# Decode attention over a key-value cache: scores as 16 rows of 512 keys, with the query as padded weight columns

## The chip, the cores and the metric

The kernel runs on one core of one Trainium2 chip. The metric is the device time in microseconds of one execution. Names of engines: PE is the tensor engine (PEld its weight loads), DVE the vector engine, ACT the scalar engine, POOL the general-purpose engine, SP the engine whose queue issues the transfers.

## What is computed

Eight sequences (B = 8) have one new token each. The model has a width of 640, 32 heads of 128 and a cache of 4096 keys and values per head. Two identical rounds (called layers 0 and 1 here) are run over the same cache:

```python
x = x + _A_ref(_layernorm(x), A_k_cache, A_v_cache, A_wq, A_wo)
x = x + _B_ref(_layernorm(x), B_w1, B_w2)
x = x + _A_ref(_layernorm(x), A_k_cache, A_v_cache, A_wq, A_wo)
x = x + _B_ref(_layernorm(x), B_w1, B_w2)
# _A_ref: q = x @ wq;  p = softmax(q . k / sqrt(128)) over 4096 keys;  o = p . v;  o @ wo
# _B_ref: relu(x @ w1) @ w2, inner width 1728
```

Everything is bf16 in memory. The cache is 537 MB; each layer needs all of it.

## The kernel before

**Visits.** A visit is one pair of heads (hp, 16 pairs) of one sequence b in one layer: 256 visits. Each has a K tile and a V tile, and each tile consists of four units (g = 0 to 3) of 512 KB, 4 KB per partition. On the chip an arena of G = 26 units holds them. For each sequence the kernel finishes layer 0, and later returns to it for layer 1; of the 128 units of a sequence, 21 stay in the arena between the two layers (the plan calls them kept) and two more are stashed in PSUM, so that layer 1 need not load them again.

**The plan.** Nothing is scheduled by a compiler. `plan()` writes out one list of operations in advance, and each engine's instructions stand in the order of that list. The order of tiles is K of visit 0, then K of visit i+1 and V of visit i in turn. Between the units of a tile, `step()` puts in small pieces of other work (chains): the softmax of a visit (T, M2, B, E, L, I), its output projection (OC, OG, O, W, Y), the rest of the layer (`finish`: norm, up, relu, down, add, norm) and the next queries (Q, QC). Where a tile can't start without a piece, `until()` puts that piece ahead of it. `feed()` writes a load into the list as soon as enough units of the arena have been given back; a load takes 1 to 8 units, depending on how far ahead the loads are by the plan's own clock. All loads go through SP's queue (L478).

**The turn.** When the last visit of layer 0 of a sequence has been done, its `finish` chain runs beside four visits of the next sequence (AHEAD = 4); then come the visits of layer 1, which start with heads 15, 14 and 13, the kept ones. While the kept units lie in the arena, five units are left for the four visits, and every load there is of one unit. There are seven such turns, one per sequence but the last.

**Scores.** A unit of K before holds 2048 keys of one head as 16 blocks of 128 keys. Each block is a weight load of 128x128 and a matmul with one column, q (L524), so the scores of a visit are a 128x64 tile, one PSUM half of `s_ps` per visit by turns. The maximum goes over the free axis (M1, L530), is transposed by a matmul with the identity (T, L534), reduced again and put on a 2x2 diagonal (M2, L538 and L540), and spread over the partitions by a matmul (B, L543). E is a scaled copy (L547) and one Exp per head (L551), which writes P as the 128x64 columns that the V matmuls need as weights. L (L556) sums P by a matmul with ones, I (L562, L566) inverts it.

**Values.** A unit of V is four matmuls with four weight columns of P each and 512 moving columns, in the four column groups of the array (`tile_position=(0, 32 * c)`, L512). Rows 32c to 32c+3 of `o_ps` hold the result; a copy (OC, L570), four matmuls that pick the right rows (OG, L575) and a scaling by 1/L (O, L585) follow.

Of the kernel before, what the change touches and what calls it, by code (L numbers as in the profile page):

```python
# [9 lines left out]
FP32 = mybir.dt.float32  # L10
# [7 lines left out]
GP = 4  # L18
# [14 lines left out]
def plan(B, NP, n_up, n_down):  # L33
# [29 lines left out]
    for i in range(NV + 1):  # L63
        pair = [("K", i)] * (i < NV) + [("V", i - 1)] * (i >= 1)
        slots += pair[::-1] if i and visits[i - 1][0] == 0 and last_of[visits[i - 1][:2]] == i - 1 else pair
    stream = []
    for which, i in slots:
        layer, b, hp = visits[i]
        stream += [(which, i, g) for g in range(UNIT) if layer == 0 or (which, hp, g) not in keep]

# [11 lines left out]
    where, kept, ready = {}, {}, {}  # L82
    ops, chains = [], []
    at = [0, 0]
# [65 lines left out]
    def take(c):  # L150

        n, op = c.pop(0)
        if op:
            ops.append(op)
            clock[0] += 0.1 + 0.03 * n
        while c and not c[0][0]:
            ops.append(c.pop(0)[1])

    def step():
# [14 lines left out]
    def query(b, n):  # L174

        return [(10, ("Q", b, order1[n])), (0, ("QC", b, order1[n]))]

    def finish(layer, b):

        norm = [(0, "sums"), (2, "mean"), (0, "center"), (2, "var"), (0, "scale"), (1, None), (1, None)]  # L180
        c = norm + [(15, ("up", k)) for k in range(n_up)] + [(0, "relu")]
        c += [(14, ("down", k)) for k in range(n_down)] + [(0, "add")]
        if layer == 0:
            c += norm
        c = [(n, op and ("C", layer, b, k, op)) for k, (n, op) in enumerate(c)]
        if layer == 0:
            c += query(b, 0) + query(b, 1)
        return c

    feed()  # L190
    for which, i in slots:
        layer, b, hp = visits[i]
        if which == "K":
            if layer == 0 and b == 0 and hp % GP == 0:
                ops.append(("Q0", hp // GP))
            if layer:
                until(("QC", b, hp))
                if order1.index(hp) + 2 < NP:
                    chains.append(query(b, order1.index(hp) + 2))
        else:  # L200
            until(("E", i))
            clock[0] = max(clock[0], ready.pop(i))
        for g in range(UNIT):
            u = find(which, i, g)
            ops.append(("mm", which, i, g, u))
            clock[0] = max(clock[0], lands[u]) + 0.5
            release(which, i, g)
            if g + 1 < UNIT:
                step()
        if which == "K":  # L210
            ops.append(("M1", i))
            ready[i] = clock[0] + 3
            step()
            chains.append([(1, ("T", i)), (0, ("M2", i)), (1, ("B", i)), (0, ("E", i)), (1, None), (1, ("L", i)), (0, ("I", i))])
        else:
# [24 lines left out]
def kernel(  # L240
# [25 lines left out]
    GW = W // UNIT  # L266
    GJ = GW // P
    VJ = NJ // UNIT
# [48 lines left out]
    nc.vector.memset(onesb_c, 1.0)  # L317
    ones_b = _free(onesb_c[:2], [(0, P)])
    ones_p = _free(onesb_c, [(0, P)])
# [3 lines left out]
    for c in range(4):  # L323
        rows = slice(32 * c, 32 * c + CJ)
        nc.vector.tensor_copy(out=gsel[rows, :, c // 2], in_=ident[rows, rows])
    eps_c = consts.tile([P, 1], FP32, name="eps_c")
    nc.vector.memset(eps_c, eps)
# [6 lines left out]
    o_ps = ps.tile([P, CJ * Dh], FP32, name="o_ps")  # L334
    s_ps = ps.tile([P, 2, 2 * NJ], FP32, name="s_ps")
    blk_ps = ps.tile([P, BANK], FP32, name="blk_ps")
# [6 lines left out]
    visits, ops = plan(B, NP, len(up_parts), DC)  # L343
    q1, s_tiles, P_tiles, m_tiles, o_tiles, blk, oy, invL, oT, nmax, st = ({} for _ in range(11))

# [160 lines left out]
    def do_mm(which, i, g, u):  # L506
        layer, b, hp = visits[i]
        at = u * GW
        if which == "V":
# [7 lines left out]
            return  # L517
        if g == 0:
            s_tiles[i] = s_ps[:, i % 2]
        h = 2 * hp + g * 2 // UNIT  # L520
        q = q1[b][:, h : h + 1] if layer else q0[:, h, b : b + 1]
        for n in range(GJ):
            j = g * GJ + n
            nc.tensor.matmul(  # L524
                s_tiles[i][:, j : j + 1], lhsT=arena[:, at + n * P : at + (n + 1) * P], rhs=q, start=True, stop=True
            )

    def do_m1(i):
        m_tiles[i] = sm.tile([P, 2], BF16, name="mrow")
        nc.vector.tensor_reduce(out=m_tiles[i], in_=s_tiles[i].rearrange("p (h j) -> p h j", h=2), axis=AX.X, op=ALU.max)  # L530

    def do_t(i):
        blk[i] = blk_ps[:, : P + 2 + 2 * NJ]
        nc.tensor.matmul(blk[i][:2, :P], lhsT=m_tiles.pop(i), rhs=ident, start=True, stop=True)  # L534

    def do_m2(i):
        hmx = sm.tile([2, 1], FP32, name="hmx")
        nc.vector.tensor_reduce(out=hmx, in_=blk[i][:2, :P], axis=AX.X, op=ALU.max)  # L538
        nmax[i] = sm.tile([2, 2], BF16, name="diag")
        nc.vector.tensor_tensor(out=nmax[i], in0=ident[:2, :2], in1=_free(hmx, [(0, 2)]), op=ALU.mult)  # L540

    def do_b(i):
        nc.tensor.matmul(blk[i][:, P : P + 2], lhsT=ones_b, rhs=nmax.pop(i), start=True, stop=True)  # L543

    def do_e(i):
        nm = sm.tile([P, 2], FP32, name="nmax")
        nc.scalar.activation(out=nm, in_=blk[i][:, P : P + 2], func=ACT.Copy, scale=-inv_sqrt_dh)  # L547
        P_tiles[i] = sm.tile([P, 2, NJ], BF16, name="P_sb", bufs=3)
        S = s_tiles.pop(i).rearrange("p (h j) -> p h j", h=2)
        for h in range(2):  # L550
            nc.scalar.activation(  # L551
                out=P_tiles[i][:, h, :], in_=S[:, h, :], func=ACT.Exp, bias=nm[:, h : h + 1], scale=inv_sqrt_dh
            )

    def do_l(i):
        nc.tensor.matmul(  # L556
            blk[i][:, P + 2 :], lhsT=ones_p, rhs=P_tiles[i].rearrange("p h j -> p (h j)"), start=True, stop=True
        )

    def do_i(i):  # L560
        L = sm.tile([P, 2], FP32, name="lsum")
        nc.vector.tensor_reduce(  # L562
            out=L, in_=blk.pop(i)[:, P + 2 :].rearrange("p (h j) -> p h j", h=2), axis=AX.X, op=ALU.add
        )
        invL[i] = sm.tile([P, 2], FP32, name="invL", bufs=3)
        nc.vector.reciprocal(out=invL[i], in_=L)  # L566

# [29 lines left out]
    def do_y(i):  # L597
# [5 lines left out]
    does = dict(load=do_load, stash=do_stash, unstash=do_unstash, weights=load_weights, mm=do_mm, M1=do_m1, T=do_t, M2=do_m2, B=do_b, E=do_e,  # L603
                L=do_l, I=do_i, OC=do_oc, OG=do_og, O=do_o, W=do_w, Y=do_y, C=do_finish, Q0=do_q0, Q=do_q, QC=take_q)

# [16 lines left out]
def _laid_out(A_x, A_k_cache, A_v_cache, A_wq, A_wo, B_w1, B_w2):  # L622
# [8 lines left out]
    w2[:Dff] = B_w2  # L631
    k = A_k_cache.reshape(B, NP, 2, Sk, Dh).transpose(0, 1, 4, 2, 3).reshape(B, NP, Dh, 2 * Sk)
    v = A_v_cache.reshape(B, NP, 2, UNIT, NJ // UNIT, p, Dh).transpose(0, 1, 5, 3, 2, 4, 6).reshape(B, NP, p, -1)
# [38 lines left out]
```

## Time and profile before

| | |
|---|---|
| runs before (3) | 2372.81, 2374.57, 2378.23 us; median 2374.57 |
| profiled execution | 2376.09 us, its span 2374.3 us |
| PE busy | 1292.5 us (54% of the span), 26486 matmuls and as many weight loads |
| DVE, ACT, POOL busy | 377.7, 355.9, 42.8 us |
| bytes moved | 996.04 MB, mean 420 GB/s |
| granted PE clock | 1.00 |

The span runs from the first to the last instruction of the core; some 1.8 us lie outside it. Busy times of engines overlap. The tables of waits say what ended the idle time of an engine, not that this time counts.

### The profile page before, as it was taken

To read this page: it belongs to the slowest core of one execution; us is meant where nothing else is said; L and a number is where in the kernel's file an instruction comes from. 1 tells how busy PE (TensorE), PEld (TensorE's weight loads), DVE (VectorE), ACT (ScalarE), POOL (GpSimd) and SP (SyncE) were. 2 spreads that over 40 slices of the span, in tenths; PEclk is the share of its full clock that TensorE was granted. 3 is DMA by queue.
4 is the path that set the end of the run, shared out by engine and by line. 5 is a ranking of instruction groups with operands and counts; after the bars stand their busy time and mean duration, and the time that the engine had idled before them with its cause. 6 is when DMAs were issued, how large, how long until landed. Compare 5 with 4: busy or idle time off the path is not lost.

```text
span 2374.3 us, 57948 instructions
## 1 busy us (share of the span) xinstructions
PE 1292.5 (54%) x26486; PEld 783.7 (33%) x26486; DVE 377.7 (16%) x1840; ACT 355.9 (15%) x1195; POOL 42.8 (2%) x198
## 2 busy tenths in 40 slices
PE   3436644476445754458454574446744466545845
PEld 2324322243223532225222352223422244223523
DVE  1102111121111211112111121112211112112211
ACT  1111211111111211112111121111211112111211
POOL 0000000000000000000000000000000000000000
DMA  9999999999999999999999999999999999999997
GB/s 411 428 429 403 428 432 431 429 398 433 428 433 427 391 433 428 433 423 404 430 434 433 406 401 431 433 431 408 420 431 430 430 408 417 431 432 410 405 434 302
DMA packets 92794, 996.04 MB, mean 420 GB/s; under 512 B 10372, under 2 KB 10372, under 8 KB 54916
## 3 DMA queue, kind: packets, MB, share of 16 engines
q1 hardware_dynamic: 92548, 992.33, 99.1%
q8 instruction: 207, 3.39, 0.5%
q14 instruction: 39, 0.32, 0.0%
HBM read 992.27 MB, written 0.01 MB: 418 GB/s over the span
## 4 chain that ended last, share of the span: by engine, by line
DMA 81%; PE 14%; DVE 2%; ACT 2%; issue 1%; POOL 1%; SPq 0%; POOLq 0%; DVEq 0%; ACTq 0%
DMA arena<-in_A_kv_dram 81%; PE o_ps L512 5%; PE s_ps L524 5%; ACT o_sb L570 1%; DVE hmx L538 1%; PE oy_ps L575 1%; PE blk_ps L496 1%; PE blk_ps L543 1%; DVE diag L540 0%; PE oy_ps L592 0%; PE blk_ps L534 0%; PE oy_ps L434 0%; DMA wq_sb<-in_A_wq_dram 0%; DVE arena L475 0%; POOL root L399 0%
## 5 line engine op out<-in xcount | busy, mean ns | idle before, releaser
L512 PE MATMUL o_ps<-arena,P_sb 128*4 128x512 bf16 x4096 | 564.8, 599 | 373.9 <-DMA arena<-in_A_kv_dram 371.6
L524 PEld LDWEIGHTS <-arena 128*128 128x128 bf16 x16384 | 501.6, 105 | 667.0 <-DMA arena<-in_A_kv_dram 660.7
L524 PE MATMUL s_ps<-q_96,arena 128*128 128x1 bf16 x8192 | 275.2, 166 | 371.9 <-DMA arena<-in_A_kv_dram 360.0
L547 ACT ACTIVATE nmax<-blk_ps 128x2 f32<-128x2 f32 x256 | 44.0, 172 | 1638.3 <-PE blk_ps L543 1638.3
L512 PEld LDWEIGHTS <-P_sb 128*4 128x4 bf16 x4096 | 90.6, 81 | 442.5 <-issue 429.4
L570 ACT CAST o_sb<-o_ps 100x512 bf16<-100x512 f32 x256 | 149.8, 585 | 228.8 <-PE o_ps L512 228.8
L562 DVE TENSOR_REDUCE lsum<-blk_ps 128x2 f32<-128x64 f32 x256 | 57.3, 224 | 588.6 <-PE blk_ps L556 588.6
L530 DVE TENSOR_REDUCE mrow<-s_ps 128x2 bf16<-128x64 f32 x256 | 57.5, 224 | 578.1 <-PE s_ps L524 542.6
L551 ACT ACTIVATE P_sb<-s_ps,nmax 128x32 bf16<-128x32 f32 x512 | 118.8, 283 | 8.2
L538 DVE TENSOR_REDUCE hmx<-blk_ps 2x1 f32<-2x128 f32 x256 | 71.4, 279 | 207.2 <-PE blk_ps L534 207.2
L556 PEld LDWEIGHTS <-onesb_c 128*128 128x128 bf16 x256 | 26.4, 103 | 199.7 <-issue 199.7
L585 DVE TENSOR_TENSOR oT<-oy_ps,invL 128x2 bf16<-128x2 f32 x128 | 20.4, 160 | 350.5 <-PE oy_ps L575 350.5
L575 PE MATMUL oy_ps<-gsel,o_sb 100*128 100x2 bf16 x1024 | 66.1, 168 | 17.5 <-ACT o_sb L570 0.7
L534 PE MATMUL blk_ps<-ident,mrow 128*2 128x128 bf16 x256 | 70.0, 274 | 3.1 <-DVE mrow L530 3.1
L543 PEld LDWEIGHTS <-onesb_c 2*128 2x128 bf16 x256 | 25.1, 98 | 125.1 <-issue 125.0
L556 PE MATMUL blk_ps<-P_sb,onesb_c 128*128 128x64 bf16 x256 | 59.7, 233 | 0.0
L575 PEld LDWEIGHTS <-o_sb 100*128 100x128 bf16 x1024 | 47.4, 106 | 33.6 <-ACT o_sb L570 29.6
L524 PE MATMUL s_ps<-q_22833,arena 128*128 128x1 bf16 x1024 | 34.1, 166 | 43.6 <-DMA arena<-in_A_kv_dram 43.4
L524 PE MATMUL s_ps<-q_18821,arena 128*128 128x1 bf16 x1024 | 33.9, 166 | 43.4 <-DMA arena<-in_A_kv_dram 43.3
L524 PE MATMUL s_ps<-q_2773,arena 128*128 128x1 bf16 x1024 | 33.9, 166 | 42.7 <-DMA arena<-in_A_kv_dram 42.7
L524 PE MATMUL s_ps<-q_14809,arena 128*128 128x1 bf16 x1024 | 34.1, 166 | 42.4 <-DMA arena<-in_A_kv_dram 41.9
L524 PE MATMUL s_ps<-q_10797,arena 128*128 128x1 bf16 x1024 | 33.9, 166 | 42.6 <-DMA arena<-in_A_kv_dram 42.5
(179 smaller groups left out, 781.2 us busy)
## 6 DMA issues: line engine op xcount, KB each, us to landing
arena<-in_A_kv_dram SPq DMA_DIRECT2D x109, 4096.0 KB, 24.8
arena<-in_A_kv_dram SPq DMA_DIRECT2D x100, 2048.0 KB, 25.2
arena<-in_A_kv_dram SPq DMA_DIRECT2D x348, 512.0 KB, 6.2
arena<-in_A_kv_dram SPq DMA_DIRECT2D x16, 2560.0 KB, 22.6
arena<-in_A_kv_dram SPq DMA_DIRECT2D x35, 1024.0 KB, 12.8
arena<-in_A_kv_dram SPq DMA_DIRECT2D x17, 1536.0 KB, 24.4
arena<-in_A_kv_dram SPq DMA_DIRECT2D x6, 3072.0 KB, 23.3
wq_sb<-in_A_wq_dram SPq DMA_DIRECT2D x4, 1280.0 KB, 30.0
```

Of the source, the lines that this page charges most:

```text
L512: nc.tensor.matmul(o_ps[32 * c : 32 * c + CJ, :], lhsT=P_tiles[i][:, h, j : j + CJ], rhs=arena[:, at + c * CJ * Dh : at + (c + 1) * CJ * D ...
L524: nc.tensor.matmul(s_tiles[i][:, j : j + 1], lhsT=arena[:, at + n * P : at + (n + 1) * P], rhs=q, start=True, stop=True)
L530: nc.vector.tensor_reduce(out=m_tiles[i], in_=s_tiles[i].rearrange("p (h j) -> p h j", h=2), axis=AX.X, op=ALU.max)
L534: nc.tensor.matmul(blk[i][:2, :P], lhsT=m_tiles.pop(i), rhs=ident, start=True, stop=True)
L538: nc.vector.tensor_reduce(out=hmx, in_=blk[i][:2, :P], axis=AX.X, op=ALU.max)
L543: nc.tensor.matmul(blk[i][:, P : P + 2], lhsT=ones_b, rhs=nmax.pop(i), start=True, stop=True)
L547: nc.scalar.activation(out=nm, in_=blk[i][:, P : P + 2], func=ACT.Copy, scale=-inv_sqrt_dh)
L551: nc.scalar.activation(out=P_tiles[i][:, h, :], in_=S[:, h, :], func=ACT.Exp, bias=nm[:, h : h + 1], scale=inv_sqrt_dh)
L556: nc.tensor.matmul(blk[i][:, P + 2 :], lhsT=ones_p, rhs=P_tiles[i].rearrange("p h j -> p (h j)"), start=True, stop=True)
L562: nc.vector.tensor_reduce(out=L, in_=blk.pop(i)[:, P + 2 :].rearrange("p (h j) -> p h j", h=2), axis=AX.X, op=ALU.add)
L570: nc.scalar.copy(out=o_tiles[i][:OR], in_=o_ps[:OR, :].rearrange("p (j d) -> p j d", j=CJ))
L575: nc.tensor.matmul(oy[i][:, :2], lhsT=o_tiles[i][:OR, j, :], rhs=gsel[:OR, j, :], start=(j == 0), stop=(j == CJ - 1))
```

## The change

Each K unit now holds 1024 keys of both heads (`_laid_out` orders the cache so on the host), as four blocks of 512 keys: two of head 0, two of head 1. The query is the weight and K moves: for each unit and block a matmul with four weight columns, of which column g is q and the other three are zero, adds into rows 32c to 32c+3 of one PSUM bank, so that after four units row 32c+g holds 512 scores. The four columns are a window into an 8-column buffer `qz` with q in column 3; POOL writes q there once per visit (`QZ`, three buffers). The maximum and Exp go over 16 rows of 512 keys (on 100 partitions, of which the others hold nothing of use); four matmuls with a selection matrix `rsel` (`PT`) turn P into the 128x64 columns of before, and a DVE copy (`PC`) takes them out of PSUM. `s_ps` is one bank instead of two halves by turns, so that K of visit i+1 is put behind E of visit i. At a turn the K and V tiles alternate by halves where the V tile came first before.

The core of the diff:

```diff
-        pair = [("K", i)] * (i < NV) + [("V", i - 1)] * (i >= 1)
-        slots += pair[::-1] if i and visits[i - 1][0] == 0 and last_of[visits[i - 1][:2]] == i - 1 else pair
+        turn = i and visits[i - 1][0] == 0 and last_of[visits[i - 1][:2]] == i - 1
+        for gs in (range(UNIT // 2), range(UNIT // 2, UNIT)) if turn else (range(UNIT),):
+            slots += [("K", i, gs)] * (i < NV) + [("V", i - 1, gs)] * (i >= 1)
...
+            pad(i)
+            if i + 1 < NV and (visits[i + 1][0] or b or hp % GP != GP - 1):
+                pad(i + 1)
+            until(("E", i - 1))
+        elif gs[0] == 0:
+            until(("PC", i))
             clock[0] = max(clock[0], ready.pop(i))
...
-            chains.append([(1, ("T", i)), (0, ("M2", i)), (1, ("B", i)), (0, ("E", i)), (1, None), (1, ("L", i)), (0, ("I", i))])
+            chains.append([(1, ("T", i)), (0, ("M2", i)), (1, ("B", i)), (0, ("E", i)), (1, None),
+                           (2, ("PT", i)), (0, ("PC", i)), (1, ("L", i)), (0, ("I", i))])
...
-        for n in range(GJ):
-            j = g * GJ + n
+        for c in range(4):
             nc.tensor.matmul(
-                s_tiles[i][:, j : j + 1], lhsT=arena[:, at + n * P : at + (n + 1) * P], rhs=q, start=True, stop=True
+                s_ps[32 * c : 32 * c + CJ, :], lhsT=qz[:, i % 3, c // 2, 3 - g : 3 - g + CJ],
+                rhs=arena[:, at + c * BANK : at + (c + 1) * BANK],
+                start=(g == 0), stop=(g == UNIT - 1), tile_position=(0, 32 * c),
             )
...
+        nc.gpsimd.tensor_copy(out=qz[:, i % 3, :, 3], in_=q)
...
-        nc.vector.tensor_reduce(out=m_tiles[i], in_=s_tiles[i].rearrange("p (h j) -> p h j", h=2), axis=AX.X, op=ALU.max)
+        nc.vector.tensor_reduce(out=m_tiles[i][:OR], in_=s_ps[:OR], axis=AX.X, op=ALU.max)
...
-        nc.tensor.matmul(blk[i][:2, :P], lhsT=m_tiles.pop(i), rhs=ident, start=True, stop=True)
+        nc.tensor.matmul(blk[i][:1, : 4 * CJ], lhsT=m_tiles.pop(i)[:OR], rhs=rsel[:OR], start=True, stop=True)
...
-        nc.vector.tensor_tensor(out=nmax[i], in0=ident[:2, :2], in1=_free(hmx, [(0, 2)]), op=ALU.mult)
...
+        for h in range(2):
+            nc.tensor.matmul(
+                blk[i][64 * h : 64 * (h + 1), 16:17], lhsT=ones_h, rhs=mx[:, h : h + 1], start=True, stop=True,
+                tile_position=(0, 64 * h),
+            )
...
-        for h in range(2):
-            nc.scalar.activation(
-                out=P_tiles[i][:, h, :], in_=S[:, h, :], func=ACT.Exp, bias=nm[:, h : h + 1], scale=inv_sqrt_dh
+        nc.scalar.activation(out=P_rows[i][:OR], in_=s_ps[:OR], func=ACT.Exp, bias=nm[:OR], scale=inv_sqrt_dh)
+
+    def do_pt(i):
+        P_row = P_rows.pop(i)
+        for k in range(BANK // P):
+            nc.tensor.matmul(
+                blk[i][:, 32 + k * 4 * CJ : 32 + (k + 1) * 4 * CJ], lhsT=P_row[:OR, k * P : (k + 1) * P],
+                rhs=rsel[:OR], start=True, stop=True,
             )
+
+    def do_pc(i):
+        P_tiles[i] = sm.tile([P, 2, NJ], BF16, name="P_sb", bufs=2)
+        nc.vector.tensor_copy(
+            out=P_tiles[i].rearrange("p h (c k) -> p h c k", k=BANK // P),
+            in_=blk[i][:, 32 : 32 + 2 * NJ].rearrange("p (k h c) -> p h c k", k=BANK // P, h=2),
+        )
```

## The prediction

> **What bounds the kernel now.** I read the page first: the queues and the chain that ended last.
>
> ```profile
> DMA packets 92794, 996.04 MB, mean 420 GB/s; under 512 B 10372, under 2 KB 10372, under 8 KB 54916
> q1 hardware_dynamic: 92548, 992.33, 99.1%
> q8 instruction: 207, 3.39, 0.5%
> DMA 81%; PE 14%; DVE 2%; ACT 2%; issue 1%; POOL 1%; SPq 0%; POOLq 0%; DVEq 0%; ACTq 0%
> ```
>
> The kernel is bound by its transfers: the data's packets fill 99.1% of sixteen engines' span, and no compute engine is above 54%. The change moves no byte of the cache more or less, so at first sight it should do nothing. The third line is the one that matters. Queue q8 brings instructions: 3.39 MB over the 2 x 26486 rows of PE are 64 bytes each, so this is PE's program, fetched in 207 packets of 16 KB, 256 instructions each. They take time on the same engines.
>
> What a fetch costs shows in a stretch of steady streaming. First its queues (the window from 902 to 1002 us):
>
> ```profile
> q1 hardware_dynamic: 1982, 43.07, 100.3%
> q8 instruction: 8, 0.13, 0.5%
> q14 instruction: 1, 0.01, 0.0%
> ```
>
> Eight fetches. A load is complete when the last of sixteen engines reports its part. The trace's stamps of these reports for loads ending at 901.00 and 1001.84 us spread over 2.41 and 3.88 us. At both ends the engines fall into two groups of eight. Each fetch throws one engine of the slow group back by about 1 us, one after the other; after eight fetches every one of the slow group has been hit once and the other group never. The mean distance of the groups went from 1.46 (896.16) to 2.79 us: 1.33 us per hit. Over 207 fetches a slow engine has 207/8 = 26 hits, 34 us. The sum agrees: the data packets' counts times the median time of each size, per engine, are 2325 us; with 34 us of fetches and 1.5 us before the first load they end at 2360.7, and the last load landed at 2359.55. So the slowest engine is busy all the time, and the end is its work plus a tail of 14.8 us (last visit, last MLP).
>
> The windows around one turn (columns: busy PE, PEld, DVE, ACT, POOL, PE clock, DMA share, GB/s):
>
> ```profile
> 1325.00:1350.00 25.00, 13.55 (x291) 8.09 (x286) 6.31 (x25) 3.67 (x12) 0.00 (x0) 1.00 1.00 425
> 1350.00:1375.00 25.00, 17.92 (x334) 11.55 (x330) 4.56 (x25) 3.90 (x14) 2.63 (x12) 1.00 0.97 364
> 1375.00:1400.00 25.00, 18.37 (x355) 11.90 (x352) 5.61 (x26) 5.48 (x16) 2.63 (x12) 1.00 1.02 388
> 1425.00:1450.00 25.00, 10.36 (x203) 5.67 (x199) 2.88 (x14) 2.76 (x10) 0.00 (x0) 1.00 1.00 430
> ```
>
> In the turn the rate falls. The slow engine does not rest there either: loads of one unit land every 1.24 us, with jumps to about 2.4 us where a fetch hits it; only the eight fast engines lose their lead, as five free units don't let them run ahead. PE is the busiest here, 18.1 of 25 us, 7.2 us per 9.92 us visit (8 units), and it has little cover. This is where the change can lose. From the timeline, the second norm of the finish chain and the first query:
>
> ```profile
> 1382.60 0.16 DVE L390 TENSOR_SCALAR root<-oy_ps 128x1 f32<-128x1 f32 x1 [0.68 <-PE oy_ps L369]
> 1386.06 0.31 POOL L375 TENSOR_SCALAR xq<-xc,rstd 128x5 bf16<-128x5 f32 x1
> 1386.70 0.41 PE L496 MATMUL blk_ps<-xq,wq_sb 128*128 128x1 bf16 x10
> 1394.20 0.54 PEld L524 LDWEIGHTS <-arena 128*128 128x128 bf16 x16
> ```
>
> POOL needs 3.8 us for the inverse root, and the first layer-1 K (1394.20) comes 7 us after its query: slack.
>
> **The change, part by part.**
>
> *K units (removed: 64 weight loads and 64 matmuls per visit; added: 16 of each).* PE's time for a unit stays: 16 matmuls of L524 took 0.56 to 0.59 us, and four 512-column matmuls in column groups, as in L512, 0.60 us (eight in 1.02). What falls is the program: per visit 128 rows become 32, PT adds 8, B adds 2, together 86 fewer, 22,016 in all. That is 86 fetches of 256 instructions. On the path, at 1.33 us per hit on one engine of eight: 86/8 x 1.33 = **-14.3 us**. Bounds: if the engines evened out, 86 x 0.93 us (median of a fetch packet) / 16 = 5.0 us; at the largest step of one hit, 1.38, it is 14.8. I take the slow engine's price, since the sum above closes with it.
>
> *Loads.* The plan writes 631 loads instead of 632, 348 of one unit in both. By the packets' medians this is under 0.1 us.
>
> *Softmax chain.* M1 reads 512 columns instead of 64: from the two reductions, 0.224 us (64) and 0.279 (128), 0.86 ns per column, so 0.61 us; the 100x512 copy L570, 0.585, is near. Exp on 100x512 also some 0.6 instead of 0.46 for two. The diagonal (0.15) goes. PT is four matmuls like L575 (0.27), PC a DVE pass over 128x64 (0.22). M1's extra 0.39 us delays T, and what is queued behind T on PE; E now ends about 2.5 us after the last K matmul, against V's four units of 2.2 us, so the next K, which needs the single bank, waits 0.2 to 0.4 us when PE works without waiting for data. A visit at full pace took 5.75 us (K at 1394.2 and 1400.0) and would take 6.3 to 6.9, beside 9.7 us of transfer for 8 units. Cover: the arena of 26 units. Cost 0 in steady stretches. If the cover were gone, 256 visits x 0.8 (between 0.55 and 1.15) = 205 us.
>
> The waits show how much PE waits for data, which is that cover:
>
> ```profile
> PE s_ps L524 <- DMA arena<-in_A_kv_dram: 625.2, 199, 7.6
> PE o_ps L512 <- DMA arena<-in_A_kv_dram: 371.6, 159, 13.0
> PEld L556 <- issue: 199.7, 247, 0.9
> PEld L543 <- issue: 125.0, 247, 0.5
> ```
>
> The last two rows show PE's loads for the untiled L waiting 0.81 us and for B 0.51 us behind column-group matmuls. The Trainium skill, TensorEngine Tiling (Array Packing), Tiling Modes, Key Properties, says that a change of the tiling mode drains the engine; PT between V and K adds such a change per visit, and by that rule, if all of it counted, 256 x 0.5 us = 128 us would make about 2490. The trace's 997 us of PE waiting for data speak for zero outside the turns.
>
> *The turn's ring.* Per visit PE gets +0.27 (PT), +0.1 (B), +0.39 (T waits), +0.4 (waiting out V before PT, as at B), +0.4 (K units to 0.60), -0.1 (T is narrower): 7.2 + 1.5 = 8.7 us of 9.92. It fits. Slots with T and a piece of the MLP reach 1.6 us against 1.24 and make PE up to 0.9 us late; four loads stand in the queue (issue to landing 5.5 us), which covers 2 to 3 us.
>
> *The finish chain comes later.* The last V tile of layer 0 now ends with the K tile beside it, four units later. In the new order the second norm's last step stands behind V unit 1 of the fourth visit ahead, with two units between it and the query; before there were two units and two more between query and K. So PE waits: the matmul of the variance, DVE, POOL's 3.8 us end 6.5 us after unit 0 landed; the query 0.41, its copy on ACT 0.16, and new, QZ on POOL (0.19 to 0.31 by POOL's rows) with three handovers of about 0.1: K starts at 7.7 instead of 4.5, a stall of **3.1 us**. Queued behind it is all of PE's work, and with it the return of units to the ring. Next: the loads in flight run dry at 9.9; K's first unit, given back at 8.3, restarts the engine 1.7 us after its issue (2.94 us to the first report of a load on an idle queue, less 1.24), at 10.0. Loss 0.1 us; with the lateness above I take 0.5. Layer 1 starts on kept units, so PE then gives back one unit per 0.6 us. Bounds: -0.5 (the halves in turn give back units earlier at the turn's start) to 2 us per turn; 7 x 0.5 = **+3.5 us**.
>
> *Tail.* The last unit lands with V's last quarter; P is ready before by either chain: 0 to 0.6, **+0.3**.
>
> **Sum.** 2376.09 - 14.3 + 3.5 + 0.3 = 2365.6 for an execution like the profiled one, which lay 1.5 us above the median of the runs: **2364 us**.
>
> **The rivals.**
>
> *Fetches even out.* If the lag of the slow engines is harmless (their time is made up elsewhere), 5.0 us are won and 3.8 given back: 2373, no change that a measurement of this kernel can tell (within 0.2%, 4.7 us). For it: only 0.5% stands in q8's row. Against it: the sum that closes.
>
> *PE becomes the bound in the turns: slower.* The ring lets PE be late by 3 us once, not by a little in every unit. It decides from 9.92 us per visit. At 10.6 (0.17 us per unit beyond my 8.7 plus the slots' unevenness and drains), over 4.3 visits and 7 turns, (10.6 - 9.92) x 4.3 x 7 = 20.5: 2374.6 - 14.3 + 20.5 = 2381. For it: nearly every slot is now a change between column groups and untiled matmuls, and the pieces of the MLP stand closer. Against it: 1.2 us spare by the sum.
>
> *No stall, nothing lost in the turns:* 2374.6 - 14.3 = 2360, inside the forecast.
>
> **How the numbers follow.** Forecast 0.68, evened-out fetches 0.16, PE-bound turns 0.16. Range 2355 to 2376: below from 14.8 us, -0.5 per turn and the lowest run (1.8 under the median), above into the first half of the slower case. Faster 0.68, same 0.16, slower 0.16.
>
> **What would show it.** q8 with 120 or 121 packets; the spread of a load's reports growing by 1.33 us per eight fetches, so about half as much from turn to turn; M1 near 0.61 us; before layer 1 of each sequence a PE wait of 2 to 4 us for the query, with landings still 1.24 us apart. I am wrong if landings in the turns go beyond 1.24 us outside hits (second rival), or if the last landing moves by under 6 us with fetches at 121 (first).

## The result, and the profile after

The changed kernel takes 2401.87 us (median of 4 runs, 2400.84 to 2405.13) where the kernel before takes 2376.40 beside it: ratio 1.0108 [1.0084, 1.0131], 25 us slower. The forecast was 12 us faster; the time lies far above the range. The profiled execution took 2405.13 us, its span 2403.3.

The page of the changed kernel, queues and chain:

```profile
DMA packets 92569, 994.67 MB, mean 414 GB/s; under 512 B 10356, under 2 KB 10356, under 8 KB 54900
q1 hardware_dynamic: 92404, 992.33, 98.8%
q8 instruction: 121, 1.98, 0.3%
DMA 74%; PE 19%; DVE 4%; issue 2%; POOL 1%; ACT 0%; DVEq 0%; SPq 0%; ACTq 0%; POOLq 0%
```

The fetches fell from 207 to 121, as forecast: the program's 86 packets are gone. Yet the same 992.33 MB took longer, and on the chain DMA gave 7% of the span to other engines. The tail did not move: from the last landing (2388.6) to the end 14.7 us, 14.8 before. So all of it was lost while data streamed.

**Where.** The end of a load is the report of the slowest of sixteen engines. I laid the landings of both kernels over the bytes they had brought in, and split the curve: seven stretches of steady streaming between the turns (620 MB in all), and the rest (the turns, start and end). Differences to the kernel before, at the 991st MB:

| kernel | steady, 620 MB | rest | sum |
|---|---|---|---|
| forecast (fetches by share; rest with +3.5) | -8.9 | -1.9 | -10.8 |
| changed | -0.8 | +29.9 | +29.0 |

The sum is firm for these two executions: it is the difference of the last landings, 2388.60 - 2359.55. The split is rough for this kernel. Its plan cuts the loads otherwise, so that only 502 of some 640 landings fall on the same byte as before, and with other edges of the stretches its steady part comes out anywhere from -4 to +20 us. By none of them were the 9 us saved where streaming is steady; by this one 30 us were lost in the rest, which the turns make up for the most part. The windows around the turn that the prediction showed (in the changed kernel it lies 15 us later; columns as there):

```profile
1365.00:1390.00 25.00, 16.53 (x178) 6.92 (x171) 5.41 (x23) 4.23 (x9) 2.99 (x14) 0.50 0.94 359
1390.00:1415.00 25.00, 19.11 (x274) 11.08 (x277) 4.76 (x24) 3.60 (x11) 3.24 (x15) 0.50 0.98 388
1415.00:1440.00 25.00, 21.33 (x238) 6.63 (x226) 7.93 (x28) 8.35 (x18) 0.77 (x4) 0.50 0.99 383
1440.00:1465.00 25.00, 13.81 (x150) 4.42 (x151) 4.07 (x18) 4.81 (x12) 0.58 (x3) 0.50 1.02 436
```

The rates of the first two are those of before (364, 388). The third stays at 383 GB/s, where layer 1 begins and PE has kept units to work on. The kernel before had recovered by then:

```profile
1400.00:1425.00 25.00, 21.27 (x485) 13.38 (x481) 5.57 (x29) 6.27 (x22) 0.00 (x0) 1.00 1.02 427
```

So some 1.1 MB, or 2.6 us at that rate, are lost in this window. The granted clock is new too (the third number from the right): 0.50.

The beginning of layer 1 in the changed kernel, from the timeline of 1408 to 1417 us (start, length, engine, line, operation; in brackets the idle time before, and what ended it):

```profile
1408.36 0.60 PE L537 MATMUL o_ps<-arena,P_sb 128*4 128x512 bf16 x4 [0.68 <-DMA arena<-in_A_kv_dram]
1410.56 0.32 POOL L400 TENSOR_SCALAR xq<-xc,rstd 128x5 bf16<-128x5 f32 x1
1410.93 0.41 PE L521 MATMUL blk_ps<-xq,wq_sb 128*128 128x1 bf16 x10 [1.77 <-POOL xq L400]
1411.64 0.19 POOL L553 COPY qz<-q_12543 128x2 bf16<-128x2 bf16 x1 [0.76 <-ACT q_12543 L529]
1411.89 0.60 PE L544 MATMUL s_ps<-arena,qz 128*4 128x512 bf16 x4 [0.55 <-POOL qz L553]
...
1415.56 0.69 DVE L500 COPY arena<-stash_ps 128x1024 bf16<-128x1024 bf16 x1 [1.10 <-PE s_ps L544]
1416.17 0.68 DVE L557 TENSOR_REDUCE mrow<-s_ps 100x1 bf16<-100x512 f32 x1
1416.90 0.08 PEld L561 LDWEIGHTS <-mrow 100*1 100x1 bf16 x1 [1.92 <-DVE mrow L557]
```

From the end of the last V unit (1408.96) to K (1411.89) 2.9 us pass, close to the stall of 3.1 that was forecast. What was not forecast is that the ring is slow to recover. The loads of this stretch were issued at 1409.00, 1412.53, 1413.95, 1415.10 and only then at 1417.58, with one or two outstanding where the kernel before had four. The next two free units go to the two stashed units, which PSUM fills and no load; and the V unit that would free the one after stands behind T, which waits for M1, which stands on DVE behind the copy out of the stash (the last three lines). In 8.6 us four loads went out where seven could have landed.

### The profile page after: what moved, and what is told of

Same layout as the page of the kernel before. It is cut to its first block, busy times and chain, and to the rows that moved or that the text cites. A ratio compares the mean times of both kernels' runs of the same rounds, so it can differ in the third digit from the quotient of the medians.

```text
span 2403.3 us, 36688 instructions
## 1 busy us (share of the span) xinstructions
PE 1386.5 (58%) x15478; PEld 497.7 (21%) x15478; DVE 461.9 (19%) x1847; ACT 411.7 (17%) x939; POOL 91.7 (4%) x454
## 3 DMA queue, kind: packets, MB, share of 16 engines
q1 hardware_dynamic: 92404, 992.33, 98.8%
## 4 chain that ended last, share of the span: by engine, by line
DMA 74%; PE 19%; DVE 4%; issue 2%; POOL 1%; ACT 0%; DVEq 0%; SPq 0%; ACTq 0%; POOLq 0%
DMA arena<-in_A_kv_dram 73%; PE s_ps L544 8%; PE o_ps L537 5%; DVE mrow L557 2%; PE blk_ps L521 1%; DVE stash_ps L491 1%; PE blk_ps L586 1%; PE blk_ps L599 1%; PE oy_ps L636 1%; PE blk_ps L572 1%; DVE lsum L606 1%; PE blk_ps L561 0%; POOL root L424 0%; ACT P_row L581 0%; PE oy_ps L459 0%
## 5 line engine op out<-in xcount | busy, mean ns | idle before, releaser
L544 PE MATMUL s_ps<-arena,qz 128*4 128x512 bf16 x4096 | 558.1, 594 | 572.9 <-DMA arena<-in_A_kv_dram 551.6
L557 DVE TENSOR_REDUCE mrow<-s_ps 100x1 bf16<-100x512 f32 x256 | 177.6, 694 | 559.7 <-PE s_ps L544 557.1
L544 PEld LDWEIGHTS <-qz 128*4 128x4 bf16 x4096 | 91.2, 83 | 637.3 <-issue 616.5
L614 ACT CAST o_sb<-o_ps 100x512 bf16<-100x512 f32 x256 | 150.0, 586 | 183.7 <-PE o_ps L537 170.7
L581 ACT ACTIVATE P_row<-s_ps,nmax 100x512 bf16<-100x512 f32 x256 | 175.9, 687 | 8.3
L593 DVE CAST P_sb<-blk_ps 128x64 bf16<-128x64 f32 x256 | 57.5, 224 | 601.4 <-PE blk_ps L586 597.1
L561 PE MATMUL blk_ps<-rsel,mrow 100*1 100x16 bf16 x256 | 47.3, 185 | 88.8 <-DVE mrow L557 88.8
L586 PE MATMUL blk_ps<-rsel,P_row 100*128 100x16 bf16 x1024 | 70.5, 179 | 9.1 <-ACT P_row L581 1.8
L521 PE MATMUL blk_ps<-xq,wq_sb 128*128 128x1 bf16 x1280 | 51.8, 165 | 38.6 <-DVE lsum L606 25.7
L636 PEld LDWEIGHTS <-wo_sb 128*128 128x128 bf16 x1440 | 50.3, 105 | 59.4 <-issue 59.4
L521 PEld LDWEIGHTS <-wq_sb 128*128 128x128 bf16 x1280 | 53.1, 104 | 45.8 <-issue 42.0
## 6 DMA issues: line engine op xcount, KB each, us to landing
wq_sb<-in_A_wq_dram SPq DMA_DIRECT2D x4, 1280.0 KB, 29.9
```

The costliest lines, as they stand in the source:

```text
L521: nc.tensor.matmul(q_ps[:, h : h + 1], lhsT=wq_sb[:, g, c, (2 * n + h) * Dh : (2 * n + h + 1) * Dh], rhs=xlns[b][:, 0, c : c + 1], start=( ...
L544: nc.tensor.matmul(s_ps[32 * c : 32 * c + CJ, :], lhsT=qz[:, i % 3, c // 2, 3 - g : 3 - g + CJ], rhs=arena[:, at + c * BANK : at + (c + 1) ...
L557: nc.vector.tensor_reduce(out=m_tiles[i][:OR], in_=s_ps[:OR], axis=AX.X, op=ALU.max)
L561: nc.tensor.matmul(blk[i][:1, : 4 * CJ], lhsT=m_tiles.pop(i)[:OR], rhs=rsel[:OR], start=True, stop=True)
L581: nc.scalar.activation(out=P_rows[i][:OR], in_=s_ps[:OR], func=ACT.Exp, bias=nm[:OR], scale=inv_sqrt_dh)
L586: nc.tensor.matmul(blk[i][:, 32 + k * 4 * CJ : 32 + (k + 1) * 4 * CJ], lhsT=P_row[:OR, k * P : (k + 1) * P], rhs=rsel[:OR], start=True, st ...
```

## The experiments

Ratios are to runs of the kernel before on the same chip, whose medians there lay between 2370.29 and 2373.82 us.

### What the fetches are worth

**before_twice** (the kernel before; the added lines only):

```diff
         for n in range(GJ):
...
+            if (5 if layer == 0 else 4) <= hp <= 11:
+                nc.tensor.matmul(
+                    s_tiles[i][:, j : j + 1], lhsT=arena[:, at + n * P : at + (n + 1) * P], rhs=q, start=True, stop=True
+                )
```

> The kernel before, with every score matmul and its weight load issued twice in 120 visits that lie in steady streaming (heads 5 to 11 in layer 0, 4 to 11 in layer 1), so that PE's program is 15,360 rows longer, 60 fetches of 16 KB, with nothing else changed. PE needs some 2 us more in each of these visits, where it waits for data anyway. By the price of the prediction (1.33 us for every eight fetches, on the slowest engine) the time rises by 10 us, 0.42%. By the mean over 16 engines (0.93 us each) it rises by 3.5 us, 0.15%. If a fetch in steady streaming is free, it stays.

2385.78 us, ratio 1.0062 [1.0049, 1.0074], +15 us (10 expected) for 60 fetches more; by the curve of landings +10.1, of it +10.7 in the steady stretches.

**before_few**:

```diff
-        for n in range(GJ):
+        for n in range(0, GJ, 4 if (5 if layer == 0 else 4) <= hp <= 11 else 1):
```

> The kernel before, with 12 of every 16 score matmuls of a K unit left out in the 120 steady visits (heads 5 to 11 of layer 0, 4 to 11 of layer 1; the output is then not the reference's): 120 x 48 x 2 = 11,520 rows of the tensor engine's program less, 45 fetches (162 instead of 207), no other change. Prediction's price (1.33 us per eight fetches on the slowest engine): 45/8 x 1.33 = -7.5 us, 0.32% faster. Rival, the fetches even out over sixteen engines: 45 x 0.93 / 16 = -2.6 us, and the rival that fewer fetches are worth nothing: 0. If -7.5 comes, the term of the prediction holds in a kernel whose transfers are otherwise the same, and the changed kernel must lose it again by something else.

2367.42 us, ratio 0.9979 [0.9970, 0.9988], -5 us (-7.5 expected) for 45 fetches less, in a kernel that leaves out three quarters of the score matmuls of those visits; by the curve -6.5, of it -6.9 steady. Together 105 fetches moved the medians by 20 us and the curve by 16.6, where the price of the prediction gives 17.5 and the mean over sixteen engines 6.1. Taken together the two runs fit the price, and not the mean; singly, the medians give 1.5 and 0.6 times of it, and the second lies midway between the price and the mean. If the price holds, the changed kernel must lose those 9 us of its steady stretches again.

### The query that comes late

**after_cap34** (the finish chain may go about five units earlier) and **after_vfirst** (the order at a turn as before):

```diff
-CAP = 20
+CAP = 34
```

```diff
-        for gs in (range(UNIT // 2), range(UNIT // 2, UNIT)) if turn else (range(UNIT),):
-            slots += [("K", i, gs)] * (i < NV) + [("V", i - 1, gs)] * (i >= 1)
+        gs = range(UNIT)
+        pair = [("K", i, gs)] * (i < NV) + [("V", i - 1, gs)] * (i >= 1)
+        slots += pair[::-1] if turn else pair
```

> The changed kernel with CAP = 34 instead of 20: more pieces of other work may stand between two units, so the finish chain of a sequence ends about five units earlier and its first query is done before the fourth visit ahead has ended. Theory A (the late query starves the ring): the wait of PE before the first layer-1 K falls from 1.8 us for the query's input plus 0.5 for POOL's copy to nearly nothing, the landings there stay about 1.24 us apart, and some 3.4 us per turn, 24 us over seven turns, come back: 2378 us. Theory B (the row-wise softmax, with its 0.69 us reduction and Exp and the single score bank, delays the units all through the turn): the pieces stand closer, units are returned no earlier, and the time stays within 2395 to 2410 us.

> The changed kernel with the turn's order as before: the whole V tile of the last layer-0 visit ahead of the next K tile. The loads are then those of the kernel before, 632 with the same sizes, and the finish chain stands two to three units earlier, with five units between the query and the first layer-1 K. In exchange the softmax of the next visit stands in one piece ahead of the second K tile (M1, T, M2, B and E behind one another, some 3 us of waiting for PE). Theory A: the loss at the start of layer 1 goes (24 us), and 0 to 2 us per turn come in at the turn's start: 2378 to 2392 us. Theory B: no gain, 2400 us or more.

2385.86, ratio 1.0065 [1.0050, 1.0079], and 2384.12, 1.0065 [1.0043, 1.0087]. By the curve the sum falls from +29.0 to +11.3 and +8.4. In after_vfirst, whose loads are cut as before, the steady part is +0.5 and the rest +7.9. PE's waits over the whole run (us in total, times, longest), changed kernel:

```profile
PE blk_ps L561 <- DVE mrow L557: 88.8, 188, 1.0
PE blk_ps L521 <- POOL xq L400: 12.5, 8, 1.8
PE s_ps L544 <- POOL qz L553: 6.2, 11, 0.6
```

and with CAP 34:

```profile
PE blk_ps L521 <- POOL xq L400: 5.3, 6, 1.2
PE s_ps L544 <- POOL qz L553: 2.4, 4, 0.6
```

In the kernel before, PE's wait for the query's input (second row) was 4.5 us:

```profile
PE blk_ps L496 <- POOL xq L375: 4.5, 7, 0.9
```

The waits for the query fall by 11 us, and the loss with them. The other two kernels are controls. **before_halves** (the kernel before with the turn's order by halves):

> The kernel before with only the turn's order changed: K and V tiles alternate by halves there, as in the changed kernel; scores and softmax as before. The query then stands directly ahead of the first layer-1 K, as after. Theory A: the order alone brings most of the loss; PE waits some 2 us for the query's input at each turn (POOL's copy of q is not there), 2 to 3 us of landings are lost per turn, 2390 to 2397 us. Theory B: the order alone does nothing, 2376 us.

2374.29, ratio 1.0015 [1.0006, 1.0024]: by itself the order costs some 4 us, without the longer chain behind it. **before_cap34** (the kernel before with CAP 34):

> Control for the run with CAP 34: the kernel before with CAP 34 instead of 20, which lets the finish chain go about five units earlier. In the kernel before the query has 7 us of slack, so nothing waits for it: 0 us, within 0.1%. If this kernel too gets faster by several us, the 17 us that CAP 34 brought the changed kernel are not the query's stall alone.

2373.73, ratio 1.0013 [1.0004, 1.0022]: no gain, 2 to 3 us lost. So CAP 34 by itself is worth nothing; what it brings the changed kernel is the earlier finish chain, with the query at its end. after_vfirst gains the same 16 us with the loads of before, so the fewer loads of CAP 34 (616 for 631) are not what brings it.

### Transfers that are slower everywhere

With the query mended the steady part still showed no gain. The records of the packets say why: from the first steady stretch to the last they were longer in the changed kernel. Medians, before and changed: 8 KB 309 and 309 (mean 310.3 and 312.8), 16 KB 611 and 613, 32 KB 1213 and 1215 ns, a fetch 935 and 1068 ns; the 4-KB packets, of which single-unit loads consist, have 159 in both and differ in the mean alone (165.6 and 170.7), and single-unit loads landed 1.24 and 1.27 us apart. My first theory blamed the denser stream of moving columns, because the granted clock had fallen along with it.

**before_vtwice** (added in the V branch; four more column-group matmuls into idle columns) and **after_knarrow**:

```diff
+            if b >= 4 and (5 if layer == 0 else 4) <= hp <= 11:
+                for c in range(4):
...
+                        idle_ps[32 * c : 32 * c + CJ, :], lhsT=P_tiles[i][:, h, j : j + CJ],
+                        rhs=arena[:, at + c * CJ * Dh : at + c * CJ * Dh + BANK - 4 * NJ],
+                        start=True, stop=True, tile_position=(0, 32 * c),
```

```diff
+        w = 32 if b >= 4 and (5 if layer == 0 else 4) <= hp <= 11 else BANK
...
-                s_ps[32 * c : 32 * c + CJ, :], lhsT=qz[:, i % 3, c // 2, 3 - g : 3 - g + CJ],
-                rhs=arena[:, at + c * BANK : at + (c + 1) * BANK],
+                s_ps[32 * c : 32 * c + CJ, :w], lhsT=qz[:, i % 3, c // 2, 3 - g : 3 - g + CJ],
+                rhs=arena[:, at + c * BANK : at + c * BANK + w],
```

> The kernel before, with a second set of four column-group matmuls of 384 moving columns (into spare columns of the scores' bank, read by nobody) for each V unit of the steady visits of sequences 4 to 7 only, that is of the second half of the run: the tensor engine then streams nearly as many moving columns in column groups as the changed kernel does. 1,920 rows more, 7 or 8 fetches, +1.3 us. Theory D (in the changed kernel every transfer is slower: single-unit loads land 1.271 us apart instead of 1.238, pairs 2.548 instead of 2.459, a fetch takes 1.068 instead of 0.935 us, and it is the denser moving stream that does it, along with the granted clock of 0.56): in the second half the granted clock falls below 1.00, the median of a fetch goes to about 1.07 us and single units land 1.27 us apart, half of the loads x 0.04 = 12 us more, +13 us in all; the first half stays as before, if the state is not carried from one execution into the next. Rival (the slower transfers come from something else in the changed kernel, such as its instruction stream, its POOL copies or its plan): clock 1.00, cadence as before, +1.3 us.

> The changed kernel, with the K matmuls of the steady visits of sequences 4 to 7 only 32 columns wide instead of 512 (the other scores are left over from an earlier visit, so the output is not the reference's); the number of instructions, the loads and the plan are those of the changed kernel. Theory D (the moving stream slows the transfers): in the second half clock back to 1.00, a fetch to 0.935 us, single units 1.238 us apart: -10 to -12 us against the changed kernel, so +14 to +16 against the one before (0.6%). Rival (something else): the cadence stays at 1.271 everywhere, and only the turns gain a little from shorter K units outside them, 0 to -2: +23 to +26 against before (1.0%).

2375.86, ratio 1.0017 [1.0006, 1.0027], and 2402.25, 1.0131 [1.0118, 1.0144]. The clock rows of the changed kernel's page, and of before_vtwice:

```profile
PEclk9999755555555555555555555555555555555555
```

```profile
PEclk9999999999999999999998555555555555555555
```

The clock does fall to half where the second half of the run streams more columns. But its packets stay as before (32 KB 1213, a fetch 933 to 940 ns in every 300 us), and the changed kernel with narrow K matmuls keeps the slow ones, and the clock of 0.50 as well. The theory falls: a half clock came without slow packets.

What differs from the start, and stays, is where the data goes. `rsel` (32 bytes per partition) and `qz` (96) are constants, and the arena is laid out behind the constants: it begins at byte 119,168 of a partition instead of 119,040 = 465 x 256. The next run moves it so in the kernel before, with nothing else:

```diff
+    shift_c = consts.tile([P, 2 * GP * B], BF16, name="shift_c")
+    nc.vector.memset(shift_c, 0.0)
     eps_c = consts.tile([P, 1], FP32, name="eps_c")
```

> The kernel before, with one idle constant of 128 bytes per partition ahead of the weights and the arena and nothing else: the arena starts at byte 119,168 of a partition, as in the changed kernel (rsel 32 bytes and qz 96 bytes stand ahead of it there), instead of 119,040 = 465 x 256. Theory S (the place of the arena slows every transfer: the changed kernel's packets are 2 to 4 ns longer whatever their size, from its first steady stretch on, and a load costs 0.03 to 0.09 us more): single-unit loads land 1.27 us apart instead of 1.238, a 32-KB packet has a median of 1,216 ns instead of 1,213, a fetch about 1.07 us instead of 0.935, clock 1.00; 632 loads x 0.035 to 0.045 = 22 to 28 us, and 207/8 x 0.13 = 3 us by the fetches, +25 to +31 in all (1.0 to 1.3%). Rival (it is the changed kernel's instructions, of whichever engine): 0 us, cadence as before. The Trainium skill, DMA: Bandwidth & Descriptors, How a descriptor splits into AXI transactions, says that a descriptor that does not start at a multiple of 256 bytes is cut at the boundary below its start and costs extra beats, which would be the mechanism of theory S.

**before_shift: 2388.49, ratio 1.0060 [1.0047, 1.0073]**, 14 us slower, granted clock 1.00: slow packets without a half clock. Fetches have a median of 1073 ns, 32 KB 1215, single units land 1.27 us apart: the changed kernel's numbers. Added up, the data's packets took 2366 us of each of the sixteen engines, where they took 2354 before. The sign and the packets are as expected; the size is half of what I expected, perhaps because adding up each landing's delay counts it also where the ring sets the pace. By the curve it is +9.2 in the steady stretches and +6.1 in the rest. Two more addresses, with 256 and with 64 idle bytes:

> The kernel before with 256 idle bytes ahead of the arena, which then starts at 119,296 = 466 x 256. Theory S (a start that is no multiple of 256 bytes costs extra at every packet): as before, ratio 1.000, 32-KB packets 1,213 ns, fetches 0.935 us. Rival (any other place than 119,040 is slower, for instance because of the weights or of a boundary further up): +14 us as with 128 bytes.

> The kernel before with 64 idle bytes ahead of the arena, which then starts at 119,104, 64 bytes past a multiple of 256. Theory S: as slow as with 128 bytes, +10 to +16 us (ratio 1.004 to 1.007), 32-KB packets 1,215 to 1,217 ns, fetches 1.05 to 1.08 us. Rival (only multiples of 128 count, or only the offset 128 is bad): ratio 1.000.

At 119,296 = 466 x 256: 2373.09, ratio 0.9999 [0.9990, 1.0009], packets as before. At 119,104: 2390.68, 1.0070 [1.0055, 1.0086], packets as at 119,168. So a start 64 or 128 bytes past a multiple of 256 costs 0.6 to 0.7%, and one at the next multiple nothing. Behind the idle bytes the weights move with the arena; they are loaded once, in the first 150 us, so the slower packets of the later stretches are the arena's. The rates of the forty slices, at 119,168 and at 119,296:

```profile
GB/s 410 428 427 399 425 430 430 426 394 431 426 432 423 392 432 426 432 414 399 429 430 429 407 410 428 429 432 404 401 429 429 428 401 417 429 429 408 405 432 295
```

```profile
GB/s 412 429 429 400 428 433 432 428 402 433 428 434 426 398 434 427 433 425 397 430 431 433 414 413 432 433 429 412 421 431 430 430 407 423 428 432 414 411 433 306
```

Little in a single slice would be noticed: 1 to 4 GB/s in 26 of the forty, more in a few (20 in one).

### The changed kernel with the arena in its old place

**after_aligned**, and the same with CAP 34 (**after_aligned_cap34**) and with the V tile first (**after_aligned_vfirst**):

```diff
     kv = ctx.enter_context(tc.tile_pool(name="kv", bufs=1))
+    late = ctx.enter_context(tc.tile_pool(name="late", bufs=1))
...
-    rsel = consts.tile([P, 4 * CJ], BF16, name="rsel")
+    rsel = late.tile([P, 4 * CJ], BF16, name="rsel")
...
-    qz = consts.tile([P, 3, 2, 8], BF16, name="qz")
+    qz = late.tile([P, 3, 2, 8], BF16, name="qz")
```

> The changed kernel, with rsel and qz put behind the arena instead of ahead of it, so that the arena and all weights stand at the addresses of the kernel before; plan, loads and instructions are unchanged. Theory S: cadence 1.238, fetch 0.935, packets 1,213 again, the granted clock 0.56 as in the changed kernel; 616 to 631 loads x 0.04 + 121/8 x 0.13 = -25 to -27 us against the changed kernel, +0 to +4 against the one before (ratio 1.000 to 1.002). Rival: no difference, ratio 1.011.

> As after_aligned, and CAP 34, so that the finish chain and with it the first query of layer 1 come five units earlier (worth -16 us in the changed kernel). If both causes add up: 2402 - 25 - 16 = 2361 us where before is 2375 (ratio 0.994): what the prediction said the change would give, and the 14 us of fetches are real. If the fetch saving was lost with the slower transfers only by chance of the same size (the fetches being worth nothing, and the turns alone costing the rest), 2372 to 2376.

> As after_aligned, with the V tile ahead of the K tile at a turn, as in the kernel before, instead of alternating halves (and CAP 20): this too brings the query back to its old place, worth -17 us in the changed kernel at equal transfers. If both add up: 2402 - 25 - 17 = 2360 us (ratio 0.994); its loads are those of the kernel before, 632 of the same sizes, so the comparison with before has only the fetches (-14.3) and the new chain in it. Rival as in the run above: 2372 to 2376.

2387.48, ratio 1.0059 [1.0047, 1.0071]; 2370.65, 0.9989 [0.9979, 0.9998]; 2371.93, 0.9987 [0.9976, 0.9998]. By the curve:

| kernel | steady, 620 MB | rest | sum |
|---|---|---|---|
| after_aligned | -10.2 | +20.6 | +10.3 |
| after_aligned_cap34 | -9.4 | +3.8 | -5.7 |
| after_aligned_vfirst | -8.0 | +4.5 | -3.5 |
| before_shift | +9.2 | +6.1 | +15.3 |
| before_few (45 fetches less) | -6.9 | +0.5 | -6.5 |

How firm are the columns? after_aligned and after_aligned_cap34 share some 500 landings with the kernel before, and their steady part moves by 10 us or more with the edges of the stretches. The kernels whose loads are cut as before (after_vfirst, after_aligned_vfirst, before_shift, before_few; over 630 shared landings) move by up to 4 when compared landing by landing, and before_shift256 and before_vtwice, which should show nothing there, give +2 or less. The rest is less firm, as a curve is one execution: before_shift256, equal to before by the medians, ends 6 us ahead of it by its curve.

So the steady part is settled by the kernels with the old cut of loads: with the arena in place the fetches bring the 9 us that the prediction gave them there (-8.0), and the misplaced arena takes just as much (+0.5 in after_vfirst, +9.2 in before_shift). And on the same chip the earlier finish chain and query are worth 2387.48 - 2370.65 = 17 us. Both mended kernels beat the kernel before by 0.1%, barely clear of the noise, and not by the 0.6% that I then expected.

### The rest of the turns

Where 5.4 us more of the fetches were due, the rest is +4 to +5: some 10 us are still lost, by this split in the turns. The medians say the same of the whole: after_aligned_vfirst is 0.5 to 5.7 us faster than before, where 14.3 were due. I tried the single bank of the scores, the longer M1, both, and CAP 34 with the V tile first, each on after_aligned_vfirst:

```diff
-            until(("E", i - 1))
+            until(("E", i - 2))
...
-    s_ps = ps.tile([P, BANK], FP32, name="s_ps")
-    blk_ps = ps.tile([P, BANK], FP32, name="blk_ps")
-    oy_ps = ps.tile([P, BANK], FP32, name="oy_ps")
+    s_ps = ps.tile([P, 2, BANK], FP32, name="s_ps")
+    one_ps = ps.tile([P, BANK], FP32, name="one_ps")
+    blk_ps, oy_ps = one_ps[:, : BANK // 2], one_ps[:, BANK // 2 :]
```

```diff
-        nc.vector.tensor_reduce(out=m_tiles[i][:OR], in_=s_ps[:OR], axis=AX.X, op=ALU.max)
+        nc.vector.tensor_reduce(out=m_tiles[i][:OR], in_=s_ps[:OR, : BANK // 8], axis=AX.X, op=ALU.max)
```

> As after_aligned_vfirst, with two banks for the scores by turns (room for the second is made by putting the two small PSUM tiles of the softmax and of the output projection into one bank), so that K of visit i+1 need only stand behind E of visit i-1, as in the kernel before. Theory B (the single bank costs the turns' starts: at a turn the second K follows the first K with no V between, and PE stands through M1, T, M2, B and Exp, some 2.9 us where a ring of five units covers 2 to 3): the jumps of 1 to 1.5 us at the starts of the turns go, -6 to -9 us against after_aligned_vfirst, about 2363 (ratio 0.995 to 0.996). Theory M (M1's extra 0.45 us and T behind it make PE late by a little at every visit of the turn): 0 to -2 us.

> As after_aligned_vfirst (one bank), with the maximum taken over the first 64 of the 512 columns only (a smaller maximum cancels in the softmax): M1 falls from 0.69 to about 0.25 us, the rest stays. Theory M: -5 to -9 us against after_aligned_vfirst, about 2364. Theory B: the stall between the two K tiles falls by 0.45 us of 2.9 per turn, -1 to -3 us in all.

> Both: two banks and the maximum over 64 columns. What is left then of the change is its fetches and PT, PC and the narrow B. If the chain explains the whole rest: 2374 - 14.3 + 0 to 1 = 2360 to 2361 (ratio 0.994). If something else is lost at the turns (the untiled matmuls of PT between column groups, or the fetches worth less than 14), 2364 to 2370.

> As after_aligned_vfirst, with CAP 34 as well. If the finish chain or the query still holds up the ring with the V tile first, -3 us or more; with the query back in its old place I expect 0 (2371 to 2373), as CAP 34 brought nothing in the kernel before.

2385.95 (1.0048 [1.0029, 1.0066]), 2370.52 (0.9982 [0.9972, 0.9992]), 2379.11 (1.0021 [1.0010, 1.0032]), 2377.31 (1.0010 [0.9998, 1.0022]). None of the gains that were hoped for came, and two banks made it slower. PE's waits with one bank (after_aligned_vfirst) and with two:

```profile
PE blk_ps L563 <- DVE mrow L559: 93.3, 199, 1.0
PE s_ps L546 <- ACT P_row L583: 10.1, 9, 2.3
```

```profile
PE one_ps L621 <- DVE lsum L608: 77.9, 247, 0.3
PE s_ps L546 <- ACT P_row L583: 10.2, 9, 2.3
```

K's wait for Exp is the same 10 us in nine times, with one bank and with two; the kernel before has 8.1 in nine. But the two small tiles, now in one, made PE wait for DVE at every visit (77.9 us, first line), so the run takes this cost along with the second bank's use, and decides nothing on the bank. The short M1 takes PE's wait for it from 93.3 to 8.7 us, but the time by the medians by 1.4 us only, with intervals that overlap, where 5 to 9 were expected; with two banks it takes 6.8 us, and the intervals still touch. CAP 34 costs the V-first kernel 5 us. So M1 may be a part of the 10 us, which is not shown, and what is lost in the turns stays open.

## Why the prediction was wrong

**Fetches, -14.3.** Right in count (121), and in price where it can be read: -8.0 us in the steady stretches of after_aligned_vfirst, where 8.9 was its share. It was hidden in the result, not absent. Whether the turns got their 5.4 us can't be told apart from what is lost there.

**What was not in the sum: the place of the arena, +14.** This is the first step that failed. The part on loads took the packets' times of before for the changed kernel ("under 0.1 us"), and 128 bytes of new constants for nothing. No row of before could show the price, but the list of what the change moves should have had the addresses, and the Trainium skill has the rule that speaks against it, which I did not weigh: DMA: Bandwidth & Descriptors, How a descriptor splits into AXI transactions, states that the first transaction of a descriptor that does not start at a multiple of 256 bytes starts at the boundary below it, and that the bytes before the start still cost beats. The page tells this of reading; here the address that was written moved. The runs agree with the boundary at four addresses (465 x 256 and 466 x 256 without the loss, 64 and 128 bytes beyond with it), and not with a cost that grows with the bytes before the start: 64 cost as much as 128. That it is this mechanism is not shown.

**The finish chain, +3.5 (0.5 per turn).** The second failed step, a term mis-sized: 17 us, 2.4 per turn, beyond the bound of 2. The stall was right (3.1, measured 2.9 at the turn shown), with QZ's part in it (0.19). Wrong was the step after it, that K's first unit restarts the engine with a loss of 0.1 us: the sum asked when the first load goes out, and not how many follow it. At the turn shown two of the next units need no load, and one waits for M1 behind the copy out of the stash; that all seven turns go so was not read.

**The turn's ring, 0.** Wrong by some 10 us, whose cause stays open. M1 took 0.694 us where 0.61 was forecast, and T waited for it 188 times, 0.47 us each, near the 0.39 counted. PE was not the bound in every unit (the second rival): single units landed 1.27 us apart as in before_shift, and 1.24 with the arena in place. The mechanism on the slower side was another one, and the rival that came nearest in sign was wrong in cause.

**Steady cover, chain, drains.** Right: Exp 0.687 (0.6), PC 0.224 (0.22), the K units 0.594 (0.60), and in steady streaming none of it cost time that can be seen (-8.0 of 8.9 us). PE still waited 835 us for data. The drains, taken as 0 there, cost nothing visible either.

**Tail, +0.3.** 14.7 against 14.8.

The sum with the runs' values: -14.3 (fetches) + 14 (arena) + 17 (query) + 10 (turns) = +27, measured +25 by the medians. The 10 are what was left over in after_aligned_vfirst, so this checks that arena and query add up, and nothing more.

## What to carry to other kernels

When a change adds a tile, however small, look where it moves the big buffers: keep what transfers write at multiples of 256 bytes, by putting small constants behind them. In a ring with little room, a stall isn't priced by the first load it delays alone; count how many loads can go out in the microseconds after it, unit by unit, and what each unit waits for. And compare landings over bytes moved, in steady and other stretches apart, before explaining a total, for kernels that cut their loads alike: a gain and a loss of 9 us each cancelled here in stretches that looked unchanged.

## What the runs showed of the hardware

- A start of 64 or 128 bytes past a multiple of 256 made packets of 16 and 32 KB 2 ns longer in the median (611 to 613, 1213 to 1215), those of 4 KB not (159), a program fetch 15% longer (935 to 1073 ns), and the whole run 0.6 to 0.7% slower.
- The granted clock fell to 0.50 some 250 us into the changed kernel, and at some 1300 us in before_vtwice, and the matmuls did not slow: in before_vtwice the column-group matmuls of V took 600 ns apiece before and 602 after the fall, those of the scores 166 and 166 (windows 700 to 1000 and 1900 to 2200 us), and sets of four of V that follow one another start 384 ns apart in both. The Trainium skill, TensorE: Matmul & The Clock Gate, What's actually happening, tells of a half clock for an idle array, half as fast as that of a busy one; here a half clock was granted after matmuls had been added, and no duration doubled. What sets it off is not shown: with narrow K matmuls in the second half (after_knarrow) it stayed at 0.50.
- A PE program fetch of 16 KB, 256 instructions, cost this transfer-bound kernel about 0.16 to 0.19 us (16.6 us by the curve or 20 by the medians for 105 of them; singly 0.26 for the 60 more and 0.11 for the 45 less), where 0.93 us on one of sixteen engines would be 0.06 in the mean.
